# Feature rows stored twice in DRAM, a new sequence of Strassen segments and a newly written instruction order in a two-block transformer kernel

## The chip, the cores and the metric

The kernel runs on one core of one Trainium2 chip. The metric is the time of one execution in microseconds on the device; the time before is 683.48 us, the median of three runs (683.15 to 684.11).

## What is computed

One pre-norm transformer layer in float32, on 2048 tokens of 448 features:

```python
h  = x + attention(layernorm(x)) @ wo        # 16 heads of 28, causal, window of 256 tokens
h2 = h + (gelu(n @ w_gate) * (n @ w_up)) @ w_down,   n = layernorm(h)    # 1792 hidden features
```

Scores are scaled by 28 ** -0.5, masked to the 256 tokens up to the query and go through a softmax. Biases and layer-norm gains are not there.

## The kernel before, in words

**Numbers in two parts.** Matmuls run in float32r. Each operand is split in a high part (`to_hi`, line 250, a copy on ACT) and a low part (`to_lo`, line 253, the difference, on DVE or POOL), and a product is built of hi*hi, lo*hi and hi*lo terms that accumulate in one PSUM bank. Of 448 features the last 64 do not fill a block of 128 rows, so the fourth block repeats 64 rows of the third, and the spare half of it carries low parts.

**Attention.** Tokens come in 16 tiles of 128, four tiles make a chunk. Heads come in four groups, and (group, chunk) pairs make 16 attention blocks. For a block PE computes scores, DVE adds the mask and takes the maximum in one custom instruction (line 692), the maximum goes back through PE (line 719) into the operands, PE computes the transposed scores, ACT their exponential (line 766), POOL cuts the edges of the window (line 779), and PE multiplies by the values (`attend`, line 798). `output` (line 837 on) multiplies by `wo` and DVE adds into `hres` (line 845). Between these stand matmuls that wait for nothing of attention: projections of q and k, values (224 columns each), and at the end the first matmuls of the feed-forward part.

**The second layer norm.** `layer_norms` and `normalise` (lines 269 and 303) compute it per tile of 128 tokens. `turn` (line 350) transposes it: DVE turns 32 by 32 squares in place in `xn`, four DMAs (line 358) write the tile to DRAM as `xn_d[t]`, features by tokens. For tiles 0 to 7 two DMAs (lines 362, 364) load it back into `xT` and ACT, then POOL or DVE, split it.

**Feed-forward.** The hidden features come in 14 tiles of 128. Tiles 0 to 3 of the first two token chunks run as plain products (`conv`, line 1084 on; the order is `FIRST`). All others run as Strassen units: a unit takes a half of the tokens, p = 0 (chunks 0 and 1) or p = 1 (chunks 2 and 3), and one hidden tile, and does 39 matmuls of 512 columns in seven products; two `down` steps of 12 matmuls of 448 columns go with it. `SEGS` (line 30) lists the units, two hidden tiles to a segment. The token sums that the seven products need are made by `combine(p, i)` (line 415), for i = 0 to 3 in each half: DMAs (line 441) load features of two tiles from `xn_d`, DVE adds them (line 460), ACT and DVE split the sums into `xT`, `X0`, `proj` and `ring`. The weight sums are made by `record` (line 909 on): a DMA (line 930) loads one hidden tile into `raw`, POOL makes the differences (line 937), ACT, DVE and POOL split them. A record is used by all units of its hidden tile in neighbouring segments; where the two halves of the tokens follow each other on the same tiles, they share it. There are three places for records and one buffer `raw`. `down` accumulates in four PSUM banks, and when a group of `down` steps on one chunk is complete, four DVE additions (line 1069) empty the banks into `hres`; the next group on these banks waits for that.

**What sets the order.** Every engine is fed in the order of one list, `PLAN`, a compressed list of numbers that was made ahead of time from the costs and the due times (`key`) in the code; `L.play` issues the operations in that order. Each engine works through its own instructions strictly in it. SP issues all DMAs. The list also holds spare transposes of `ident` on PE (line 1306), which compute nothing that is used.

## Time and profile before

| what | value |
|---|---|
| median of 3 runs | 683.48 us |
| the profiled execution | 680.14 us |
| its span, first to last instruction | 678.4 us |
| busy: PE, DVE, ACT, POOL | 665.5, 504.8, 396.8, 299.9 us |
| instructions of PE, DVE, ACT, POOL | 4074, 1278, 765, 459 |
| mean granted TensorE clock | 0.997 |
| DMA, mean over the span | 132 GB/s |

The numbers of the profile are of one execution, which was 3.34 us shorter than the median. PE's busy time counts a matmul from its issue to its modelled end, and neighbouring matmuls overlap, so a matmul's own duration (about 380 ns for 512 columns) is longer than its distance to the next, and a short gap between two matmuls does not show as idle time.

The stages lie as follows in the span: loads and the first layer norm from 0 on, attention blocks from about 60 to 304 us, plain feed-forward products to about 360 us, Strassen units to the end.

### The profile page before, as it was taken

How to read it: one execution, taken by the hardware profiler on the slowest of the kernel's cores; microseconds unless marked ns; L12 is line 12 of the kernel's file. 1: busy time of each engine (PE TensorE's matmuls, PEld its weight loads, DVE VectorE, ACT ScalarE, POOL GpSimd, SP SyncE). 2: the span in 40 equal slices, each digit the busy share in tenths (PEclk: the TensorE clock that was granted, in tenths of full speed). 3: DMA queues.
4: the chain of work that ended last, by engine and by line, in shares of the span. 5: the costliest groups of instructions: out<-in, count | busy, mean ns of one | idle time of the engine just before them, and what ended most of it. 6: DMA issues, size and time to landing. Idle time of an engine off the chain costs nothing.

```text
span 678.4 us, 11973 instructions
## 1 busy us (share of the span) xinstructions
PE 665.5 (98%) x4074; PEld 592.7 (87%) x4074; DVE 504.8 (74%) x1278; ACT 396.8 (58%) x765; POOL 299.9 (44%) x459
## 2 busy tenths in 40 slices
PE   8999999999999999999989999999999999999997
PEld 7998878888889877778878999999999999999997
DVE  7898789977688979977988899876566355545554
ACT  5766578774867698886455655634554443433431
POOL 3632524543444488756433474256554442122200
PEclk9999999999999999999998999999999999999999
DMA  7888866464747687544534434121212201101202
GB/s 268 267 254 250 265 185 210 140 213 135 236 131 255 180 210 221 125 119 105 150 98 95 102 85 128 57 91 39 67 53 70 74 15 52 52 7 62 110 0 109
DMA packets 92951, 89.66 MB, mean 132 GB/s; under 512 B 35225, under 2 KB 82009, under 8 KB 92889
## 3 DMA queue, kind: packets, MB, share of 16 engines
q1 hardware_dynamic: 92888, 88.89, 44.2%
q8 instruction: 32, 0.52, 0.3%
q14 instruction: 31, 0.25, 0.1%
HBM read 59.51 MB, written 29.36 MB: 131 GB/s over the span
## 4 chain that ended last, share of the span: by engine, by line
PE 88%; DVE 7%; DMA 2%; issue 1%; ACT 1%; SPq 1%; POOL 0%; DVEq 0%; ACTq 0%
PE bank L248 81%; PE bank L798 6%; DVE bank L692 2%; DVE v L460 1%; DMA v<-xn 1%; PE bank L314 1%; DMA pp<-in_wv_dram 1%; DVE xT L254 1%; DVE X L254 1%; SPq L441 0%; DVE proj L254 0%; PE bank L719 0%; DVE hres L1069 0%; DVE mhl L712 0%; DVE xn L823 0%
## 5 line engine op out<-in xcount | busy, mean ns | idle before, releaser
L248 PE MATMUL bank<-xT,proj 128*128 128x512 f32 x620 | 171.1, 384 | 0.0
L692 DVE CUSTOM_DVE_ANT_0 bank<-bank,mask 128x384 f32<-128x384 f32 (+2 forms) x256 | 131.6, 551 | 24.0 <-PE bank L248 22.0
L248 PE MATMUL bank<-ring 84*128 84x384 f32 (+6 forms) x618 | 136.3, 311 | 2.4 <-DVE mx L692 1.0
L248 PE MATMUL bank<-xT,ring 128*128 128x512 f32 x536 | 134.8, 379 | 0.0
L248 PE MATMUL bank<-ring,proj 128*128 128x448 f32 x628 | 128.9, 356 | 2.5 <-DVE hres L1069 2.5
L248 PEld LDWEIGHTS bank<-ring,proj 128*128 128x128 f32 x628 | 119.6, 190 | 5.8 <-ACT xT L251 2.9
L248 PEld LDWEIGHTS bank<-xT,proj 128*128 128x128 f32 x620 | 113.6, 190 | 11.4 <-DVE mhl L709 0.2
L766 ACT ACTIVATE pp<-bank 128x384 f32<-128x384 f32 (+1 forms) x212 | 103.3, 533 | 21.6 <-PE bank L248 18.4
L248 PEld LDWEIGHTS bank<-ring 128*128 128x128 f32 (+1 forms) x618 | 103.5, 190 | 13.7 <-DVE mx L692 2.4
L248 PEld LDWEIGHTS bank<-xT,ring 128*128 128x128 f32 x536 | 101.1, 189 | 13.1 <-DVE v L1013 0.6
L779 POOL TENSOR_SCALAR_AFFINE_SELECT pp<-pp 128x512 f32<-128x512 f32 x120 | 73.9, 642 | 56.1 <-ACT pp L766 55.2
L1069 DVE TENSOR_TENSOR hres<-bank,hres 128x448 f32<-128x448 f32 x72 | 42.7, 618 | 33.0 <-PE bank L248 32.9
L248 PE MATMUL bank<-proj,xT 128*128 128x224 f32 x352 | 60.8, 274 | 0.3 <-ACT proj L251 0.2
L937 POOL TENSOR_TENSOR raw<-raw 64x128 f32<-64x128 f32 (+1 forms) x90 | 48.3, 549 | 28.7 <-DMA raw<-in_halves_dram 25.4
L254 DVE TENSOR_TENSOR proj<-v,proj 128x512 fp32r<-128x512 f32 (+1 forms) x56 | 40.2, 725 | 23.9 <-ACT proj L251 23.5
L248 PEld LDWEIGHTS bank<-proj,xT 128*128 128x128 f32 x352 | 52.9, 191 | 2.3 <-ACT proj L251 0.7
L251 ACT ACTIVATE proj<-v 128x512 fp32r<-128x512 f32 (+1 forms) x56 | 32.8, 601 | 36.0 <-DVE v L1039 32.4
L254 POOL TENSOR_TENSOR ring<-raw,ring 128x256 fp32r<-128x256 f32 (+2 forms) x42 | 38.3, 920 | 35.2 <-ACT ring L251 34.5
L251 ACT ACTIVATE ring<-bank 8x512 fp32r<-8x512 f32 x64 | 37.4, 585 | 26.8 <-PE bank L719 25.5
L1013 DVE TENSOR_TENSOR v<-v,bank 128x512 f32<-128x512 f32 x48 | 32.8, 684 | 26.2 <-PE bank L248 23.6
L248 PE MATMUL bank<-wos,ohl 128*128 128x448 f32 x192 | 49.4, 359 | 0.3 <-DVE mx L692 0.2
L248 PE MATMUL bank<-X,ring 128*128 128x512 f32 x146 | 48.2, 379 | 0.0
(117 smaller groups left out, 955.7 us busy)
## 6 DMA issues: line engine op xcount, KB each, us to landing
ring<-k SPq DMA_DIRECT2D x44, 336.0 KB
raw<-in_halves_dram SPq DMA_DIRECT2D x18, 640.0 KB
ring<-q SPq DMA_DIRECT2D x32, 336.0 KB
q<-proj SPq DMA_DIRECT2D x15, 448.0 KB
k<-proj SPq DMA_DIRECT2D x11, 448.0 KB
hres<-in_x_dram SPq DMA_DIRECT2D x16, 224.0 KB
xn<-xn SPq DMA_DIRECT2D x64, 56.0 KB
ge<-in_halves_dram SPq DMA_DIRECT2D x16, 224.0 KB
```

The lines of the kernel that those rows point to most:

```text
L248: nc.tensor.matmul(o.rearrange("p (t h) -> p t h", h=2), w, mixed(m), **how)
L251: nc.scalar.activation(dst, src, AF.Copy)
L254: (eng or nc.vector).tensor_sub(dst, src, f(hi))
L314: nc.tensor.transpose(bank[b.k][:, n * 128:(n + 1) * 128], xn[i2][:, o:o + 128], ident)
L460: op("dve", 0.07 + n * 0.00104, 0.17 + n * 0.00104, key, lambda: nc.vector.tensor_tensor(out, a, b, op=op_), [*ar, *br, "mtfree"], w, port ...
L692: nc.vector.tensor_tensor_reduce(at, at, plain(mask[:, o:384]), 1.0, -BIG, OP.add, OP.max, mx[i // 2][:, i % 2, j:j + 1])
L766: nc.scalar.activation(pp[:, j:j + per, o * 128:o * 128 + n].rearrange("p j (h t) -> p j h t", h=2), bank[b.k][:, 0:n * per].rearrange("p ...
L779: nc.gpsimd.affine_select(a, a, pattern=[[0, 4], [-cm, 128]], compare_op=op_, fill=0.0, base=0, channel_multiplier=cm)
L798: nc.tensor.matmul(bank[b.k][32 * j:32 * j + DH + 1, lo * 128:(hi + 1) * 128], v[:, 4 * c - 2 + m, g % 2, j, :], pp[:, j, at[m] * 128:(at[ ...
L937: op("pool", 0.14 + n * 0.00215, 0.18 + n * 0.00215, key, lambda: nc.gpsimd.tensor_tensor(out, a, b, op=OP.subtract), [*ar, *br], w, port= ...
L1013: op("dve", 0.605, 0.702, key, lambda: nc.vector.tensor_tensor(plain(out), plain(a), unmixed(bank[bs[i].k]), op=OP.add), ar, w, bs[i])
L1069: op("dve", 0.533, 0.626, key + 3 * q + 3, lambda t=t, b=banks[q]: nc.vector.tensor_tensor(plain(hres[:, t, :]), unmixed(bank[b.k][:, 0:D] ...
```

## The change

Five things are changed:

1. **Twice the rows.** The buffer `xn` becomes 512 wide (`xw`), and ACT writes the tile's first 64 features in front of all 448 of them, in two instructions (`norm_twice`), so that `xn_d[t]` holds 512 rows: features 0 to 63, then 0 to 447. DVE turns 512 columns. The four DMAs that write a tile have runs of the same length and 16 squares where they had 14.
2. **Loads of `combine`.** All blocks that the sums need are now plain slices of those rows: one load for the first tile of a pair, where there were three, and four for the second, where there were five. The weights' rows are laid out to fit (`four`, `turned`). In `turn` the last block goes through a small buffer `last` in `ring`, which the DMA of line 373 now writes, and ACT needs two instructions where it needed three.
3. **`SEGS`.** All ten units of the first half of the tokens come first, then the fourteen of the second. Only hidden tiles 12 and 13 are still shared, so 22 records are made where there were 18. There are fewer groups of `down` steps, so that line 1069 (now 1078) runs 64 times, not 72.
4. **Splits at the start.** The low parts of the first value weights and of the first q/k weight tile are made on POOL, where they were made on DVE.
5. **`PLAN`, due times and planner costs.** The list is a new one. `LN2` and the second entry of `XK` (the due time of the second half's sums) are later. PE has 36 spare transposes, where it had 30; its other matmuls are the same in number and size.

`MOVED` now bounds the tiles of the first layer norm that go through DRAM; at 16 there are none, so that this way is taken by the second layer norm alone, as before.

```diff
-SEGS = ((0, (4, 5)), (0, (6, 7)), (0, (8, 9)), (1, (8, 9)), (1, (6, 7)), (1, (4, 5)), (1, (0, 1)), (1, (10, 11)), (0, (10, 11)), (0, (12, 13)), (1, (12, 13)), (1, (2, 3)))
+SEGS = ((0, (4, 5)), (0, (6, 7)), (0, (8, 9)), (0, (10, 11)), (0, (12, 13)), (1, (12, 13)), (1, (10, 11)), (1, (8, 9)), (1, (6, 7)), (1, (4, 5)), (1, (0, 1)), (1, (2, 3)))
...
-LN2 = (120, 10)
-XK = ((0, 10), (240, 10))
+LN2 = (180, 10)
+XK = ((0, 10), (360, 10))
...
-    xn_d = [dram.tile([D, 128], F32, name=f"xn{t}") for t in range(NT)]
+    xn_d = [dram.tile([512, 128], F32, name=f"xn{t}") for t in range(NT)]
...
+        def norm_twice():
+            for n, o in ((64, 0), (D, 64)):
+                nc.scalar.activation(xw[i2][:, o:o + n], hres[:, t, 0:n], AF.Identity, scale=bnve[:, 1, i4:i4 + 1],
+                                     bias=bnve[:, 2, i4:i4 + 1])
...
-        dma(key + 0.1, 230, lambda: nc.sync.dma_start(f(xT[:, 4:7, c]), d[0:384].rearrange("(b p) t -> p b t", p=128)),
+        last_at = span("ring", 10240, 128)
+        dma(key + 0.1, 230, lambda: nc.sync.dma_start(f(xT[:, 4:7, c]), d[128:512].rearrange("(b p) t -> p b t", p=128)),
             put, [XT(t)])
-        dma(key + 0.1, 80, lambda: nc.sync.dma_start(f(xT[:, 3, c]), d[D - 128:D]), put, [("xt3", t)])
+        dma(key + 0.1, 80, lambda: nc.sync.dma_start(last, d[0:128]), put, [last_at])
...
-            load(slice(0, 128), 0, 2, d[0:256].rearrange("(k p) t -> p k t", k=2), 0)
-            last = d[384:448].rearrange("(k p) t -> p k t", k=1)
             if not k:
-                load(LOW, 2, 2, some(d, 2, 2), 1)
-                load(HIGH, 2, 2, some(d, 2, 3)[:, 0::2], 2)
+                load(slice(0, 128), 0, 4, d.rearrange("(k p) t -> p k t", k=4), 0)
             else:
-                load(LOW, 3, 1, some(d, 2, 2)[:, 1:2], 1)
-                load(LOW, 4, 2, some(d, 2, 2), 2)
-                load(HIGH, 4, 2, some(d, 2, 2), 3)
-                load(HIGH, 2, 2, last.to_broadcast([64, 2, 128]), 4)
+                load(slice(0, 128), 3, 3, d[128:512].rearrange("(k p) t -> p k t", k=3), 0)
+                load(slice(0, 128), 0, 1, d[0:128], 1)
+                load(HIGH, 1, 2, d[128:256].rearrange("(k p) t -> p k t", k=2), 2)
+                load(LOW, 1, 1, d[128:192], 3)
...
-            op("dve", 0.54, 0.63, key + 1, lambda b=b: to_lo(wv[:, 1, b:b + 2], wv_raw[p][:, b:b + 2], wv[:, 0, b:b + 2]),
+            eng, name = (nc.vector, "dve") if p else (nc.gpsimd, "pool")
+            op(name, 0.54 if p else 1.1, 0.63 if p else 1.15, key + 1, lambda b=b, eng=eng: to_lo(
+                wv[:, 1, b:b + 2], wv_raw[p][:, b:b + 2], wv[:, 0, b:b + 2], eng),
                [WVRAW(p, b, 2), WV(0, b, 2)], [WV(1, b, 2)], port=True)
...
 PLAN = (
-    "c-pPEW3(nc)HWEWQb-|H)wXThwr$(CZQHhO+qP|M`t3gbeBaEPHS=TU)Vh;OvT^Mzd)G-IV1NS*2%x{;!0#6Re*Zg$zgOVz2mg^lzklp^3xBsb"
...
```

What the list does to each engine's instructions is seen in their order. Tiles 0 to 15 of `xn_d` are named `xn_118` to `xn_133` there.

**SP, the loads for the third pair of tiles of the first half** (tiles 2 and 6, `xn_120` and `xn_124`), just before the plain feed-forward products end. Before:

```order
L441 DMA v<-xn_124 64x2x128
L441 DMA v<-xn_123 64x2x128
L358 DMA xn_129<-xn_85 32x14x32 x2
L441 DMA v<-xn_124 64x128
L358 DMA xn_126<-xn_80 32x14x32
L441 DMA v<-xn_120 64x2x128
L441 DMA v<-xn_124 64x2x128 x2
L441 DMA v<-xn_124 128x2x128
L441 DMA v<-xn_120 64x2x128
L441 DMA v<-xn_120 128x2x128
```

Now:

```order
L450 DMA v<-xn_124 128x128
L450 DMA v<-xn_125 128x128
L450 DMA v<-xn_124 64x2x128
L450 DMA v<-xn_124 128x3x128
L450 DMA v<-xn_124 64x128
L450 DMA v<-xn_120 128x4x128
```

Eight loads of the pair have become five, and no write of a later tile stands among them. From the first to the last load of the first half's four pairs there are 20 loads, 4 writes of tiles and 2 loads of weights, where there were 32 loads, 10 writes and 3 loads of weights; the writes of `xn_129` and `xn_128` come behind.

**DVE, up to the additions that empty the four `down` banks before the first Strassen unit** (`hres` from banks 138 to 141). Before:

```order
L460 TENSOR_TENSOR v<-v 128x128
L460 TENSOR_TENSOR v<-mask,v 128x2x128
L460 TENSOR_TENSOR v<-v 64x128 x2
L254 TENSOR_TENSOR proj<-ge,proj 128x512
L254 TENSOR_TENSOR X_3702<-v,xT 128x2x128
L460 TENSOR_TENSOR v<-v 128x128 x2
L1069 TENSOR_TENSOR hres<-bank_138,hres 128x448
L1069 TENSOR_TENSOR hres<-bank_139,hres 128x448
L1069 TENSOR_TENSOR hres<-bank_140,hres 128x448
L254 TENSOR_TENSOR X_3702<-v,xT 128x128
L254 TENSOR_TENSOR X_3702<-v,xT 128x2x128
L1069 TENSOR_TENSOR hres<-bank_141,hres 128x448
```

Now:

```order
L466 TENSOR_TENSOR v<-mask,v 128x2x128
L255 TENSOR_TENSOR proj<-ge,proj 128x512
L466 TENSOR_TENSOR v<-v 128x128
L255 TENSOR_TENSOR X_3708<-v,xT 128x2x128
L466 TENSOR_TENSOR v<-v 64x128
L255 TENSOR_TENSOR X_3708<-v,xT 128x128 x2
L255 TENSOR_TENSOR xT<-v,xT 64x128
L1078 TENSOR_TENSOR hres<-bank_138,hres 128x448
L1078 TENSOR_TENSOR hres<-bank_139,hres 128x448
L1078 TENSOR_TENSOR hres<-bank_140,hres 128x448
L1078 TENSOR_TENSOR hres<-bank_141,hres 128x448
```

The work of `combine` still stands ahead of the four additions. Between the first addition of the group before and the first of this one 74 instructions stood, and now 71: a `BN_STATS`, a `BN_AGGR`, the two transposes of the second layer norm, one split of 512 columns and one addition on 64 rows are gone from it, and one split each of 2x128 and 128 columns on 128 rows and of 128 columns on 64 rows have come in.

**PE, between the thirteenth and the fourteenth `attend`** (`bank<-ring` are scores, `bank<-proj,xT` are values of the second half of the heads, which wait for nothing of attention). Before:

```order
L248 MATMUL bank_135<-ring 128x384
L248 MATMUL bank_140<-ring 128x384
L248 MATMUL bank_134<-ring 128x384
L248 MATMUL bank_137<-ring 128x384
L248 MATMUL bank_141<-ring 128x384
L248 MATMUL bank_135<-ring 128x384
L248 MATMUL bank_136<-ring 128x384
```

Now:

```order
L249 MATMUL bank_136<-ring 128x384
L249 MATMUL bank_140<-proj,xT 128x224 x2
L249 MATMUL bank_141<-ring 128x384
L249 MATMUL bank_140<-proj,xT 128x224
L249 MATMUL bank_135<-proj,xT 128x224 x2
L249 MATMUL bank_137<-ring 128x384
L249 MATMUL bank_140<-proj,xT 128x224 x2
```

Matmuls that need nothing of attention have moved from the middle blocks to the last ones. Between the twelfth and the sixteenth `attend` stood 44 of 512 columns and 11 of 224; now there are 70 and 59.

More of the change, by code (lines that the diff above doesn't have):

```diff
@@ L169, in block_kernel @@
     one_r = pool.tile([128, 128], F32R, name="one")
[L170 removed]
+    xw = [o_m, pool.tile([128, 512], F32, name="xn1")]
+    xn.append(xw[1][:, 0:D])
     qk_d = [[[dram.tile([GF, 3, 512], F32, name=f"{'qk'[i]}{g}_{c}") for i in range(2)] for c in range(CS)]
             for g in range(NG)]
[L174 removed]
+    xn_d = [dram.tile([512, 128], F32, name=f"xn{t}") for t in range(NT)]
     bank = [psum.tile([128, 512], F32, name=f"bank{i}") for i in range(8)]
@@ L193, in block_kernel @@
     xT = xT_m.rearrange("p (b t) -> p b t", b=7)
-    last_hi = ring_m[:, 10240:10368]
+    last = f(ring_m[:, 10240:10368])
     rq_m, rk_m = ring_m[:, 0:4096], ring_m[:, 4096:10240]
@@ L256, in dma @@
     def dma(key, size, fn, r=(), w=(), after=()):
-        cost = 0.63 if size in (32, 64, 128) else 0.52 if size == 150 else 0.46 if size < 240 else 0.4
+        cost = 0.62 if size in (32, 64) else 0.52 if size in (128, 150) else 0.46 if size < 240 else 0.42
         return op("sp", cost, 0, key, fn, r, w, size=size, after=after)
@@ L303, in normalise @@
     def normalise(t, key, kind):
-        moved = kind == "ln2" and t >= MOVED
-        i2, i4 = (t % 2 if t > 7 else 1) if moved else t % 2 if t < 4 else 1, t % 4
+        moved = kind == "ln2" or t >= MOVED
+        i2, i4 = t % 2 if t < 4 and kind == "ln1" or t > 7 and kind == "ln2" else 1, t % 4
         b = None if moved else Bank(kind)
@@ L337, in normalise @@
             op("pool", 1.0, 1.1, key, norm_pool, [HR(t), ("bnve", i4)], [("xn", i2)], port=True)
+        elif moved:
+            op("act", 0.88, 0.95, key, norm_twice, [HR(t), ("bnve", i4)], [("xn", i2)])
         else:
@@ L358, in turn @@
             dma(key, 150, lambda dst=dst, src=src: nc.sync.dma_start(dst, src), [at], [("xnd", t, a)])
-        if t > 7:
+        if kind == "ln2" and t > 7:
             return
         put = [("xnd", t, a) for a in range(4)]
-        dma(key + 0.1, 230, lambda: nc.sync.dma_start(f(xT[:, 4:7, c]), d[0:384].rearrange("(b p) t -> p b t", p=128)),
+        last_at = span("ring", 10240, 128)
+        dma(key + 0.1, 230, lambda: nc.sync.dma_start(f(xT[:, 4:7, c]), d[128:512].rearrange("(b p) t -> p b t", p=128)),
             put, [XT(t)])
-        dma(key + 0.1, 80, lambda: nc.sync.dma_start(f(xT[:, 3, c]), d[D - 128:D]), put, [("xt3", t)])
-        eng = nc.gpsimd if t in TURNED else nc.vector
+        dma(key + 0.1, 80, lambda: nc.sync.dma_start(last, d[0:128]), put, [last_at])
+        on_pool = kind == "ln1" or t in TURNED
+        eng = nc.gpsimd if on_pool else nc.vector
         def hi():
             to_hi(xT[:, 0:3, c], f(xT[:, 4:7, c]))
-            to_hi(last_hi[64:128], f(xT[64:128, 3, c]))
-            to_hi(xT[0:64, 3, c], f(xT[64:128, 3, c]))
+            to_hi(xT[:, 3, c], last)
         def lo():
             to_lo(xT[:, 4:7, c], f(xT[:, 4:7, c]), xT[:, 0:3, c], eng)
-            to_lo(xT[64:128, 3, c], f(xT[64:128, 3, c]), last_hi[64:128], eng)
-        op("act", 1.1, 1.2, key + 0.2, hi, [("xt3", t)], [XT(t), span("ring", 10240, 128)])
-        op("pool" if t in TURNED else "dve", 1.6 if t in TURNED else 0.8, 1.7 if t in TURNED else 0.88, key + 0.2, lo,
-           [XT(t), span("ring", 10240, 128)], [XT(t)], port=True)
+            to_lo(xT[64:128, 3, c], last[64:128], xT[64:128, 3, c], eng)
+        op("act", 0.8, 0.9, key + 0.2, hi, [last_at], [XT(t)])
+        op("pool" if on_pool else "dve", 1.6 if on_pool else 0.8, 1.7 if on_pool else 0.88, key + 0.2, lo,
+           [XT(t), last_at], [XT(t)], port=True)
     LOW, HIGH = slice(0, 64), slice(64, 128)
@@ L431, in two @@
             return T[k].rearrange("p (b t) -> p b t", t=128)[:, n:n + step + 1:step]
-        def some(src, *ks):
-            return src[128 * ks[0]:128 * ks[0] + 64 * ks[1]].rearrange("(k p) t -> p k t", k=ks[1])
         for k in range(2):
@@ L491, in combine @@
         add(256, two(0, 0, 2), at(0, 0, 2), E, e, two(0, 0, 2), at(0, 0, 2), key + 2)
-        parts_of(4, both(1), at(1, 0, 1, 2, 3), 2, key + 2)
-        add(128, b(0, 1), at(0, 1), b(0, 1), at(0, 1), b(0, 0), at(0, 0), key + 2)
-        add(128, b(0, 3, LOW), at(0, 3), b(0, 3, LOW), at(0, 3), b(0, 2, LOW), at(0, 2), key + 2)
+        parts_of(4, both(1), at(1, 2, 3, 4, 5), 2, key + 2)
+        add(128, b(0, 3), at(0, 3), b(0, 3), at(0, 3), b(0, 2), at(0, 2), key + 2)
+        add(128, b(0, 1, LOW), at(0, 1), b(0, 1, LOW), at(0, 1), b(0, 0, LOW), at(0, 0), key + 2)
         parts_of(2, both(0), at(0, 0, 1, 2, 3), 2, key + 2)
@@ L1467, in layout @@
               for n in range(0, F, 128)]
-    ffn = [np.concatenate([rows(gate[:, n:n + 128]).reshape(128, 512), rows(up[:, n:n + 128]).reshape(128, 512),
+    ffn = [np.concatenate([turned(gate[:, n:n + 128]).reshape(128, 512), turned(up[:, n:n + 128]).reshape(128, 512),
                            inputs["B_w_down"][n:n + 128]], axis=1) for n in range(0, 128 * GC, 128)]
```

293 lines of the change are left out of this document (150 added, 143 removed).

## The prediction

> **What bounds the kernel now.** I read the busy times by stage first, in stretches of 20 us. The columns behind the stretch are its length, then the busy time of PE, PE's weight loads, DVE, ACT and POOL, the granted clock of PE, and DMA.
>
> ```profile
> core 0: us, PE busy (x) PEld busy (x) DVE busy (x) ACT busy (x) POOL busy (x), PEclk, DMA share, GB/s
> 0.00:20.00 20.00, 17.30 (x110) 15.61 (x111) 16.12 (x37) 12.06 (x18) 8.38 (x28) 1.00 0.78 264
> ...
> 200.00:220.00 20.00, 20.00 (x156) 18.36 (x156) 16.23 (x52) 15.47 (x34) 9.55 (x12) 1.00 0.72 234
> ...
> 240.00:260.00 20.00, 19.17 (x154) 16.16 (x156) 16.50 (x51) 17.32 (x36) 16.34 (x23) 1.00 0.83 224
> 260.00:280.00 20.00, 19.05 (x177) 14.28 (x177) 19.24 (x67) 18.07 (x38) 16.99 (x24) 1.00 0.77 205
> 280.00:300.00 20.00, 19.47 (x142) 16.05 (x140) 17.94 (x52) 17.12 (x37) 11.93 (x22) 1.00 0.48 114
> ...
> 340.00:360.00 20.00, 17.46 (x81) 15.67 (x80) 18.09 (x49) 10.95 (x20) 6.58 (x10) 0.94 0.29 76
> 360.00:380.00 20.00, 20.00 (x94) 17.79 (x93) 14.86 (x29) 11.53 (x21) 9.52 (x15) 0.98 0.46 107
> ...
> 440.00:460.00 20.00, 20.00 (x100) 18.49 (x99) 15.71 (x26) 8.69 (x17) 11.74 (x18) 1.00 0.25 78
> 460.00:480.00 20.00, 20.00 (x99) 18.36 (x98) 11.94 (x19) 9.71 (x19) 13.99 (x21) 1.00 0.14 46
> ...
> 660.00:680.00 20.00, 14.38 (x75) 13.64 (x73) 9.01 (x15) 2.27 (x4) 0.00 (x0) 0.96 0.24 93
> ```
>
> PE has next to no room. Its idle time is 2.70 us at the start, 20 - 14.38 = 5.62 us in the last row, of which 1.6 us lies behind the span's end at 678.4 and 4.02 us before it, 2.54 us between 340 and 360, and 0.83 + 0.95 + 0.53 = 2.31 us between 240 and 300. A change that leaves PE's matmuls as they are can give only what lies in the middle of these. The chain of work that ended last says the same of the end: from 356.59 us on it is PE alone.
>
> ```profile
> 356.59 316.48 PE bank L248 x1529
> 673.09 1.69 DVE hres L1069 x3
> ```
>
> So I looked at the stall in front of it in stretches of 3 us, and then at who was late there, on DVE's timeline (start, duration, instruction, idle time before it).
>
> ```profile
> 354.00:357.00 3.00, 0.46 (x3) 0.44 (x3) 3.00 (x9) 1.86 (x4) 1.56 (x1) 1.00 0.00 0
> 357.00:360.00 3.00, 3.00 (x12) 2.72 (x11) 2.97 (x7) 1.89 (x4) 0.72 (x1) 0.58 0.07 22
> 360.00:363.00 3.00, 3.00 (x14) 2.59 (x13) 2.94 (x8) 1.74 (x3) 0.89 (x1) 0.85 0.00 0
> ```
>
> ```profile
> 324.39 0.62 DVE L1069 TENSOR_TENSOR hres<-bank,hres 128x448 f32<-128x448 f32 x1
> ...
> 328.15 0.75 DVE L460 TENSOR_TENSOR v<-v 128x256 f32<-128x256 f32 x2 [0.35 <-DMA v<-xn]
> ...
> 344.43 0.42 DVE L254 TENSOR_TENSOR X<-v,xT 128x256 fp32r<-128x256 f32 x1 [0.96 <-ACT xT L251]
> ...
> 347.14 0.69 DVE L1115 TENSOR_TENSOR ge<-bank,ge 128x512 f32<-128x512 f32 x1 [0.59 <-ACT ge L1112]
> ...
> 355.83 1.67 DVE L1069 TENSOR_TENSOR hres<-bank,hres 128x448 f32<-128x448 f32 x3
> ```
>
> PE waits 2.54 us for the four additions of line 1069, because DVE does the token sums of `combine` first. Behind it the clock is at 0.58 for 3 us and at 0.85 for another 3, which loses 3 x 0.42 + 3 x 0.15 = 1.71 us. The whole stall costs 2.54 + 1.71 = 4.25 us. The chain goes through SP's issues and the landing of the loads here, and SP's timeline shows why.
>
> ```profile
> 324.46 0.60 SPq L441
> 325.11 0.59 SPq L441
> 325.75 2.38 DMA v<-xn
> ```
>
> ```profile
> 319.44 2.55 SPq L441 DMA_DIRECT2D v<-xn  x4
> ...
> 333.12 4.51 SPq L441 DMA_DIRECT2D v<-xn  x7
> ...
> 341.53 4.32 SPq L441 DMA_DIRECT2D v<-xn  x7
> ...
> 348.40 0.36 SPq L930 DMA_DIRECT2D raw<-in_halves_dram  x1
> ...
> 367.82 0.35 SPq L930 DMA_DIRECT2D raw<-in_halves_dram  x1
> ...
> 382.07 0.35 SPq L930 DMA_DIRECT2D raw<-in_halves_dram  x1
> ...
> 395.56 0.36 SPq L930 DMA_DIRECT2D raw<-in_halves_dram  x1
> ...
> 407.71 0.33 SPq L930 DMA_DIRECT2D raw<-in_halves_dram  x1
> ```
>
> A load takes about 0.62 us of SP (4.51 / 7 = 0.64, 4.32 / 7 = 0.62), so that the 32 loads of the first half's sums are 20 us of SP's time ahead of the last of these sums.
>
> **The loads and the stall before the units.** In the new order 20 loads stand there: 12 x 0.62 = 7.4 us less on SP, and 6 writes and one weight load fewer between them. The last sums can start some 7 us sooner, so DVE is what decides. From the addition at 324.39 to that at 355.83 DVE takes 31.44 us. What leaves this stretch and what comes in is priced by these groups.
>
> ```profile
> L284 DVE BATCH_NORM_STATS2 bnst<-hres 128x6 f32<-128x448 f32 x32 | 19.4, 617 | 1.7 <-DMA hres<-in_x_dram 1.4
> L354 DVE STREAM_TRANSPOSE xn<-xn 128x448 f32<-128x448 f32 x16 | 10.2, 638 | 0.8 <-ACT xn L309 0.8
> L254 DVE TENSOR_TENSOR proj<-ge,proj 128x512 fp32r<-128x512 f32 x6 | 4.3, 724 | 0.0
> L254 DVE TENSOR_TENSOR X<-v,xT 128x256 fp32r<-128x256 f32 x28 | 11.7, 429 | 1.1 <-ACT xT L251 1.0
> ```
>
> Out go 0.62 + 2 x 0.64 + 0.72 = 2.62 us, in comes 0.43 us; of the smaller ones two go and two come, which I set against each other. That makes 31.44 - 2.19 = 29.25 us. The idle 0.35 + 0.96 + 0.59 = 1.90 us in the stretch is what late loads and ACT cause, so 27.35 us if all of it goes. PE is held up no more if DVE takes 31.44 - 2.54 = 28.90 us. The two ends lie on both sides of that, by 0.35 us to the bad and 1.55 us to the good; I take the stall as gone. A rest of 0.35 us would not cost clock: the stretch from 240 to 260 us has 0.83 us of idle at a clock of 1.00. The Trainium skill's page TensorE: Matmul & The Clock Gate, Part 1: The HAM clock gate, says that the clock is halved after an idle window of about 3.4 us. By that page a wait of 2.54 us would cost no clock, and the sum would be 1.71 us poorer; the trace has the clock at 0.58 behind it, and the measurement decides. **-4.25 us**, between -3.9 and -4.25.
>
> **Filling the last attention blocks.** Between 240 and 300 us DVE is busy 53.7 of 60 us and PE idles for 2.31 us. By the new order 26 more matmuls of 512 columns and 48 more of 224 stand between the twelfth and the sixteenth `attend`. At 100 matmuls of mostly 512 and 448 columns in 20 us, and half of that for 224 columns, this is 26 x 0.2 + 48 x 0.1 = 10 us of PE work that waits for nothing, many times the idle 2.31. It is missing in the blocks before; one of their stretches, from 200 to 220 us, has PE at 20.00 and DVE at 16.23. At best more than 2.31 us comes back, as gaps shorter than a matmul's record don't show; at worst the idle time moves to the middle blocks and nothing comes back. I take the shown **-2.31 us**.
>
> **Spare transposes.** Six more, priced by seven at the start:
>
> ```profile
> 7.25 0.93 PE L1306 MATMUL bank<-ident 128*128 128x128 f32 x7
> ```
>
> 6 x 0.13 = **+0.8 us** if all lie where PE is busy, nothing if they lie in waits; I take the dear end.
>
> **Splits on POOL at the start.** Two of 448 columns and one of 512.
>
> ```profile
> L254 DVE TENSOR_TENSOR proj<-pp,proj 128x448 fp32r<-128x448 f32 x2 | 1.3, 626 | 0.1
> L254 POOL TENSOR_TENSOR wos<-raw,wos 128x448 fp32r<-128x448 f32 x4 | 4.6, 1145 | 5.2 <-ACT wos L251 5.2
> ```
>
> POOL takes 0.52 us longer for one, so PE, which wants the low parts after seven matmuls with the high ones, could wait 3 x 0.52 = 1.6 us; DVE is freed of 3 x 0.63 = 1.9 us in a stretch in which it is busy 16.12 of 20 us, while POOL has 11.6 us to spare. From -1.9 to +1.6, I take **0**, since neither is shown to end a wait.
>
> **Work beside PE.** `norm_twice` adds a short ACT instruction per tile and line 368's function loses one, DVE turns 64 columns more; none is near PE's chain after 360 us. Eight fewer additions of line 1069 free DVE there. The four records more are the one thing that could reach PE (third rival); in the stretches from 440 to 480 us, where one record goes with each unit, POOL is at 11.74 and 13.99 of 20 us and PE at 20.00. **0**. Later sums of the second half lighten DVE between 360 and 430 us, which covers nothing that PE waits for.
>
> **The sum.** -4.25 - 2.31 + 0.8 = -5.76, so 680.14 - 5.76 = 674.4 us for an execution like the profiled one. That one is 3.34 us under the median, with nothing in the trace to say why; I carry this over: 683.48 - 5.76 = **677.7 us**. Changes within 0.2% (1.4 us) a measurement of this kernel can hardly tell from none.
>
> **The rivals.**
> - **The stall stays on DVE.** The order still has nearly all of `combine` ahead of the four additions: 71 instructions where there were 74. For it: DVE was idle for 1.90 us only of 31.44. Against it: the 2.19 us that are gone from the stretch. If half a microsecond of the wait goes and the clock falls all the same: -0.5 - 2.31 + 0.8 = -2.0, 681.5 us. Chance 0.15, of which 0.04 within the bound.
> - **The idle time moves within attention.** Ten microseconds of filler are taken from the middle blocks. Nothing comes back: -4.25 + 0.8 = -3.45, 680.0 us. Chance 0.15. Both together: -0.5 + 0.8, 683.8 us, no change. Chance 0.07.
> - **Records fall behind the units: slower.** Ten units in a row now need a new record each, where the first six did. The loads of `raw`, issued once the record before is done with it, stand at 367.82, 382.07, 395.56, 407.71: 14.25, 13.49 and 12.15 us apart. A unit with its `down` steps is 63 matmuls at 0.2 us, 12.7 us. If records keep the 13.9 us of the first two intervals, four more fall 4 x 1.2 = 4.9 us behind, in two waits of about 2.5 us that each cost 1.71 us of clock as well: 8.3 us, and 677.7 + 8.3 = 686.0 us. It decides once the intervals stay over 12.7 us. Against it: DVE, on which the records' splits wait, has less of `combine` to do there. Chance 0.13.
>
> That the loads or segments are not what they say can't be: the built order has 40 loads for 64 and 22 records for 18.
>
> **How the numbers follow.** The forecast has the remaining 0.50. Faster: 0.50 + 0.11 + 0.15 = 0.76; same: 0.04 + 0.07 = 0.11; slower: 0.13. The range goes up to 683.8, the case of no gain, and leaves the record case out. Below, all idle time between 20 and 360 us could go and some that doesn't show: the forecast less 1.9 us at the start, 0.8 us of transposes and some 3 us in gaps that are hidden, 672.0 us.
>
> **What would show it.** Right: PE at 3.00 of 3 us in the stretches around the first unit, the clock at 1.00 there, the additions in front of it no later than PE's last matmul, loads on SP ending well ahead of the sums, DVE less full and PE fuller between the twelfth and the sixteenth block. Wrong: DVE still full up to those additions, waits of PE on DVE's line 701 in the middle blocks, or PE waiting on ACT or POOL writing `ring` or `proj` between 390 and 490 us, with loads of `raw` over 13 us apart.

## The result, and the profile after

The changed kernel takes 675.45 us (median of 4 runs, 674.98 to 677.31) against 683.32 us (682.15 to 684.11, 4 runs): a ratio of 0.9891, 95% interval 0.9867 to 0.9916. Its profiled execution took 674.99 us with a span of 673.3 us, 5.15 us less than the one before. With the experiments the kernel before was run again and had medians of 681.8 (18 runs), 681.99 (17) and 681.41 us (12); against these the changed kernel's 675.45 us is 6.0 to 6.5 us less. The changed kernel was not run again there, so its variants are compared with it by their ratios to the kernel before, each known to about 0.002, which is 1.4 us.

The busy times by stage, with the columns of the prediction's first fence:

```profile
0.00:20.00 20.00, 17.41 (x107) 15.65 (x107) 15.02 (x32) 11.53 (x18) 12.72 (x31) 1.00 0.76 258
...
200.00:220.00 20.00, 20.00 (x150) 18.35 (x146) 17.47 (x54) 13.22 (x27) 9.34 (x12) 1.00 0.68 210
...
240.00:260.00 20.00, 20.00 (x157) 17.93 (x155) 16.89 (x48) 16.43 (x35) 15.14 (x21) 1.00 0.76 211
260.00:280.00 20.00, 19.22 (x156) 15.90 (x156) 15.44 (x51) 18.57 (x40) 15.06 (x24) 1.00 0.86 225
280.00:300.00 20.00, 19.94 (x139) 15.81 (x138) 17.11 (x52) 15.02 (x34) 11.52 (x18) 1.00 0.37 92
...
340.00:360.00 20.00, 19.97 (x97) 17.83 (x96) 18.54 (x49) 10.15 (x20) 5.27 (x9) 1.00 0.23 69
360.00:380.00 20.00, 20.00 (x97) 18.06 (x97) 14.76 (x26) 12.94 (x25) 9.84 (x18) 1.00 0.56 134
...
660.00:680.00 20.00, 8.72 (x47) 8.36 (x45) 6.33 (x11) 0.94 (x2) 0.00 (x0) 0.94 0.24 92
```

The stall has gone: between 340 and 360 us PE idles for 0.03 us, not 2.54, and the clock is at 1.00 there and behind. Between 240 and 300 us the idle time is 0.78 + 0.06 = 0.84 us, not 2.31. The chain of waits now has PE alone from 305.48 us on, where it began at 356.59:

```profile
305.48 25.79 PE bank L249 x126
331.31 21.32 PE bank L249 x102
352.66 314.75 PE bank L249 x1529
667.43 1.69 DVE hres L1078 x3
```

The additions in front of the first unit, on DVE's timeline (line 1069 is 1078 now), with the idle time of DVE between the first addition of the group before and the four of this group:

```profile
323.68 1.14 DVE L1078 TENSOR_TENSOR hres<-bank,hres 128x448 f32<-128x448 f32 x2
...
342.15 0.63 DVE L255 TENSOR_TENSOR X<-v,xT 128x128 fp32r<-128x128 f32 x2 [0.38 <-ACT xT L252]
...
346.83 0.29 DVE L255 TENSOR_TENSOR X<-v,xT 128x128 fp32r<-128x128 f32 x1 [0.25 <-ACT xT L252]
...
351.89 2.22 DVE L1078 TENSOR_TENSOR hres<-bank,hres 128x448 f32<-128x448 f32 x4
```

Between these two marks DVE takes 351.89 - 323.68 = 28.21 us, where it took 31.44; this time is called the stretch from here on. DVE's idle time in it is 0.63 us, where it was 1.90, and its busy time (the third of the busy times in these rows, the kernel before first) 27.07 us, where it was 28.97:

```profile
324.39:355.83 31.44, 29.41 (x142) 26.35 (x140) 28.97 (x74) 15.38 (x29) 12.47 (x18) 1.00 0.46 123
323.68:351.89 28.21, 28.17 (x137) 25.45 (x136) 27.07 (x72) 15.42 (x31) 7.75 (x12) 1.00 0.26 77
```

The additions are only just in time. The first one ends at 352.52 us and PE's next matmul starts at 352.66, 0.15 us later, as it does in the profiles of e4, e7, e8, e9 and e10, also where their timelines name a write of ACT as what PE waited for. It starts 0.39 us after the matmul before it, where its neighbours stand 0.19 us apart.

The loads on SP (line 450) and the records' loads (line 939):

```profile
321.75 19.92 SPq L450 DMA_DIRECT2D v<-xn  x13
...
364.46 0.35 SPq L939 DMA_DIRECT2D raw<-in_halves_dram  x1
...
376.75 0.34 SPq L939 DMA_DIRECT2D raw<-in_halves_dram  x1
389.93 0.36 SPq L939 DMA_DIRECT2D raw<-in_halves_dram  x1
404.46 0.35 SPq L939 DMA_DIRECT2D raw<-in_halves_dram  x1
416.35 0.34 SPq L939 DMA_DIRECT2D raw<-in_halves_dram  x1
```

The last thirteen loads of the first half are spread over 20 us with gaps between them. The records' loads stand 12.3, 13.2, 14.5 and 11.9 us apart from 364 us on, and PE is at 20.00 in the stretches there.

### The profile page after: what moved, and what is told of

It is laid out like the page before. It is cut to its first block, busy times and chain, and to the rows that moved or that the text cites. A ratio compares the mean times of both kernels' runs of the same rounds, so it can differ in the third digit from the quotient of the medians.

```text
span 673.3 us, 12063 instructions
## 1 busy us (share of the span) xinstructions
PE 664.0 (99%) x4080; PEld 592.8 (88%) x4080; DVE 512.1 (76%) x1287; ACT 406.3 (60%) x793; POOL 322.6 (48%) x506
## 4 chain that ended last, share of the span: by engine, by line
PE 95%; DVE 2%; DMA 1%; ACT 1%; issue 0%; POOL 0%; SPq 0%; DVEq 0%
PE bank L249 87%; PE bank L807 6%; PE bank L320 1%; DVE bank L701 1%; DMA hres<-in_x_dram 1%; DMA raw<-in_wqk_dram 1%; ACT pp L775 0%; PE bank L728 0%; DVE hres L1078 0%; PE bank L1315 0%; POOL proj L255 0%; ACT proj L252 0%; ACT ring L252 0%; DVE xn L835 0%; SPq L510 0%
## 5 line engine op out<-in xcount | busy, mean ns | idle before, releaser
L249 PE MATMUL bank<-xT,proj 128*128 128x512 f32 x648 | 181.9, 386 | 0.2 <-ACT proj L252 0.2
L249 PE MATMUL bank<-ring 128*128 128x384 f32 (+7 forms) x629 | 139.9, 311 | 1.4 <-DVE mx L701 1.2
L249 PEld LDWEIGHTS bank<-xT,proj 128*128 128x128 f32 x648 | 118.1, 190 | 13.2 <-issue 0.6
L249 PE MATMUL bank<-xT,ring 128*128 128x512 f32 x508 | 127.5, 379 | 0.0
L249 PEld LDWEIGHTS bank<-xT,ring 128*128 128x128 f32 x508 | 95.9, 189 | 12.4 <-ACT ge L1121 0.4
L946 POOL TENSOR_TENSOR raw<-raw 64x128 f32<-64x128 f32 (+1 forms) x110 | 53.5, 498 | 35.5 <-DMA raw<-in_halves_dram 31.3
L249 PE MATMUL bank<-proj,xT 128*128 128x224 f32 x352 | 69.8, 272 | 0.0
L249 PEld LDWEIGHTS bank<-proj,xT 128*128 128x128 f32 x352 | 58.2, 191 | 1.9 <-ACT v L252 0.2
L255 POOL TENSOR_TENSOR ring<-raw,ring 128x256 fp32r<-128x256 f32 (+2 forms) x48 | 41.8, 878 | 34.8 <-ACT ring L252 32.3
L1078 DVE TENSOR_TENSOR hres<-bank,hres 128x448 f32<-128x448 f32 x64 | 37.5, 617 | 14.8 <-PE bank L249 14.7
```

The lines of the kernel that those rows point to most:

```text
L249: nc.tensor.matmul(o.rearrange("p (t h) -> p t h", h=2), w, mixed(m), **how)
L255: (eng or nc.vector).tensor_sub(dst, src, f(hi))
L946: op("pool", 0.14 + n * 0.00215, 0.18 + n * 0.00215, key, lambda: nc.gpsimd.tensor_tensor(out, a, b, op=OP.subtract), [*ar, *br], w, port= ...
L1078: op("dve", 0.533, 0.626, key + 3 * q + 3, lambda t=t, b=banks[q]: nc.vector.tensor_tensor(plain(hres[:, t, :]), unmixed(bank[b.k][:, 0:D] ...
```

## The experiments

**What sets the stall.** The theory is the prediction's: DVE's work in the stretch is what has to fit into PE's time. The rivals are the place of the four additions alone, and SP's loads alone.

`e1_adds_first`: the kernel before, with another order on DVE only (its rows, from the built order):

```
+L254 TENSOR_TENSOR proj<-ge,proj 128x512
 L460 TENSOR_TENSOR v<-v 64x128 x2
...
 L460 TENSOR_TENSOR v<-mask,v 128x2x128
+L1069 TENSOR_TENSOR hres<-bank_138,hres 128x448
+L1069 TENSOR_TENSOR hres<-bank_139,hres 128x448
+L1069 TENSOR_TENSOR hres<-bank_140,hres 128x448
+L1069 TENSOR_TENSOR hres<-bank_141,hres 128x448
 L460 TENSOR_TENSOR v<-v 64x128 x2
-L254 TENSOR_TENSOR proj<-ge,proj 128x512
...
-L1069 TENSOR_TENSOR hres<-bank_138,hres 128x448
```

> The kernel before, with its four additions of line 1069 ahead of the first unit moved six places forward on VectorE (and the last low part of the ninth feed-forward step before them, since the next matmuls read it). Theory (all of VectorE's work up to the first unit is late, not just the additions): the additions are in time, PE passes 353.7 without its 2.54 us wait, but the sums that were passed over are what the unit reads from its ninth matmul on, and VectorE is done with them at about 362 as before; PE waits there instead, 2.5 to 3.2 us. Time within 1 us of the kernel before, ratio 0.9985 to 1.0015. Rival (the place of the additions alone): the wait and its clock loss go, 4.25 us less, ratio 0.994, and no other wait appears.

685.05 us, ratio 1.0045 (1.0029 to 1.0062): slower. PE's timeline, which is some 4 us later here than in the profile before:

```profile
358.80 2.51 PE L248 MATMUL bank<-ring,proj 128*128 128x448 f32 x12 [1.07 <-DVE hres L1069]
361.14 1.03 PE L248 MATMUL bank<-xT,proj 128*128 128x512 f32 x4
362.01 0.38 PE L248 MATMUL bank<-X,proj 128*128 128x512 f32 x1
362.42 1.13 PE L248 MATMUL bank<-xT,proj 128*128 128x512 f32 x4
365.49 0.70 PE L248 MATMUL bank<-X,proj 128*128 128x512 f32 x2 [1.94 <-DVE X L254]
```

The additions still cost 1.07 us, and then the first unit waits 1.94 us after its ninth matmul for the sums that were passed over, 3.01 us together where 2.54 were. The rival falls. The time came out worse than the theory said, and most of that arises ahead of the rows that were moved: by the starts of the same matmuls in both profiles this execution is 3.91 us behind the profile before at 320 us already, 1.7 us of it by a stretch at half clock at 274 us. From 320 to 390 us it loses 1.36 us more. Why it came later up to 320 us is not shown; the instructions and their order are the same there, yet none of the six executions was under 684 us.

`e2_three_loads_out`: the kernel before with 40 loads.

```diff
+                skip = (k, part) in ((0, 2), (1, 1), (1, 4))
-                dma(key, (64 if rows.stop - rows.start == 128 else 32) * n, lambda: nc.sync.dma_start(
+                dma(key, (64 if rows.stop - rows.start == 128 else 32) * n, lambda: skip or nc.sync.dma_start(
```

> The kernel before with three of the eight loads of every pair of token sums left out (three sums read old data), so 40 loads for 64, in the old order. Theory (VectorE's own work decides): at most the 1.90 us that VectorE idled in the stretch come back, the wait in front of the first unit is still 0.6 us or more, 0 to 2.5 us less, ratio 0.9963 to 1. Rival (SyncE's loads decide): the stall goes as in the changed kernel, 4.25 us less, ratio 0.994 or under.

680.86 us, ratio 0.9987 (0.9969 to 1.0004). The additions come 30.65 us after the first one, not 31.44:

```profile
324.84 0.62 DVE L1070 TENSOR_TENSOR hres<-bank,hres 128x448 f32<-128x448 f32 x1 [0.30 <-PE bank L248]
...
355.49 1.67 DVE L1070 TENSOR_TENSOR hres<-bank,hres 128x448 f32<-128x448 f32 x3
```

PE waits 1.67 us. So the loads alone are worth 0.8 us of DVE's stretch, and no difference in time that this measurement resolves. The theory holds, and SP's loads alone do not decide.

`e3_eight_loads`: the changed kernel with 64 loads.

```diff
+                def go(out=out, src=src, n=n):
+                    if n < 3:
+                        nc.sync.dma_start(out, src)
+                        return
+                    for c in (slice(0, 2), *(slice(m, m + 1) for m in range(2, n))):
+                        nc.sync.dma_start(out[:, c], src[:, c])
-                dma(key, (64 if rows.stop - rows.start == 128 else 32) * n, lambda: nc.sync.dma_start(out, src), put,
+                dma(key, (64 if rows.stop - rows.start == 128 else 32) * n, go, put,
```

> The changed kernel with each pair's two large loads cut into three and two, so eight loads again for five, same bytes, same order. Theory: SyncE has idle time among these loads in the new order, VectorE stays in time to within its margin; 0 to 0.7 us more, ratio 1.000 to 1.001 against the changed kernel (0.989 to 0.990 against the kernel before). Rival (the loads were the gain): the 2.5 us wait comes back with its clock loss, 4.25 us more, ratio to the kernel before 0.995.

675.23 us, ratio 0.9897 (0.9876 to 0.9918): as the changed kernel. The stretch is 353.33 - 325.06 = 28.27 us. In the new order eight loads do as well as five.

`e7_lighter_dve`: the kernel before with less of DVE's work.

```diff
-        op("dve", 0.56, 0.65, key, lambda: nc.vector.transpose(xb, xb), [at], [at], port=True)
+        m = 64 if t in (10, 13) else D
+        op("dve", 0.56, 0.65, key, lambda: nc.vector.transpose(xb[:, 0:m], xb[:, 0:m]), [at], [at], port=True)
...
+            out = p == 0 and i > 1
-            sub(128, lambda: hi[HIGH, 0, 1], src[HIGH, 0, 1], hi[HIGH, 0, 1], [*r, *w[1]], XS(p, q, 1, i), key, 0.1)
+            sub(128, lambda: hi[HIGH, 0, 1], src[HIGH, 0, 1], hi[HIGH, 0, 1], [*r, *w[1]], XS(p, q, 1, i), key, 0.1, out)
```

> The kernel before with some 2.9 us of VectorE's work left out of the stretch ahead of the first unit, all 64 loads and the order as they are: two transposes of 448 columns are cut to 64 columns (0.53 us less each) and the six small subtractions of 64 rows of the third and fourth pair of the first half are left out (about 0.3 us each), so that the sums and some normalised rows are wrong. Theory (VectorE's work ahead of the additions sets the stall): PE's wait of 2.54 us falls to 0 to 0.5 us, the half clock behind it goes, 2.0 to 4.3 us less, ratio 0.994 to 0.997. Rival (loads or ScalarE set it): the wait stays above 2 us, ratio 0.999 to 1.

680.41 us, ratio 0.998 (0.9964 to 0.9996). The stretch is 354.44 - 324.62 = 29.82 us, and PE waits 1.05 us:

```profile
324.62 0.62 DVE L1071 TENSOR_TENSOR hres<-bank,hres 128x448 f32<-128x448 f32 x1
...
354.44 1.67 DVE L1071 TENSOR_TENSOR hres<-bank,hres 128x448 f32<-128x448 f32 x3
```

```profile
324.62:354.44 29.82, 29.52 (x144) 26.69 (x142) 27.24 (x72) 15.62 (x29) 10.82 (x18) 1.00 0.48 126
```

The wait lies between the theory's 0.5 us and the rival's 2 us. The edit took less out of the stretch than was meant: DVE is busy for 27.24 us there, 1.73 us less, not 2.9. Each of the two transposes became 0.41 us shorter (0.64 to 0.23 us), and only three of the six small subtractions stand in the stretch. Of these 1.73 us 1.62 came back. The miss is in the size of the edit, not in the mechanism.

`e9_loads_and_dve`: the edits of e2 and e7 together.

> The kernel before with both: three of eight loads of every pair left out, and the 2.9 us of VectorE's work ahead of the first unit left out (sums and some normalised rows are wrong). Alone they took 0.7 and 1.3 us off PE's wait of 2.54 us; VectorE still idled about 1.5 to 2 us for ScalarE. Theory (both feed one row of VectorE work that is late): together the wait falls to 0.6 us or less, no half clock behind it, 2.5 to 4 us less, ratio 0.994 to 0.9965. Rival (a third thing of the new order is needed, ScalarE's place or an earlier begin of the sums): more than 0.6 us of wait is left, ratio 0.997 or more.

678.25 us, ratio 0.9948 (0.9926 to 0.997), in the range that the theory gave. The stretch is 29.62 us (additions at 325.12 and 354.74), and 0.70 us of wait is left before the additions, 0.80 with a short one behind, a little more than the 0.6 us set. So the ratio is the theory's and the wait is on the rival's side: what still differs from the new order is mostly DVE's idle time for ACT, 0.95 + 1.00 us here and 0.63 us there. The mean clock was 0.999 or 1.000 in all seven executions.

`e10_heavier_dve`: the changed kernel with 1.6 us more on DVE.

```diff
+                def go():
+                    for _ in range(2 if out is E and not p else 1):
+                        nc.vector.tensor_tensor(out, a, b, op=op_)
```

> The changed kernel with the first addition of each of the four pairs of the first half made twice (same result), 4 x 0.41 us = 1.6 us more on VectorE ahead of the first unit. Theory (VectorE has no room there): the four additions come 0.9 to 1.6 us later and PE waits for them that long, without half clock, ratio to the kernel before 0.9905 to 0.992. Rival (there is room): no wait over 0.3 us, ratio as the changed kernel's, 0.989 to 0.990.

676.64 us, ratio 0.9928 (0.9913 to 0.9944): a little above the theory's 0.992, which the interval takes in, and outside the rival's range. The stretch grew by 0.74 us to 28.95, since DVE's idle time of 0.63 us took up part of the new work, and PE waits 0.39 us at 333 us and 0.48 us for the four additions:

```profile
325.67 1.14 DVE L1081 TENSOR_TENSOR hres<-bank,hres 128x448 f32<-128x448 f32 x2
...
354.62 2.22 DVE L1081 TENSOR_TENSOR hres<-bank,hres 128x448 f32<-128x448 f32 x4
```

`e4_adds_late` and `e4a_adds_little_late`: the changed kernel with its four additions five and three instructions later on DVE. The rows of the second:

```
-L1078 TENSOR_TENSOR hres<-bank_138,hres 128x448
...
 L255 TENSOR_TENSOR X_3708<-v,xT 128x2x128
 L1124 TENSOR_TENSOR ge<-bank_136,ge 128x512
 L255 TENSOR_TENSOR xT<-mask,xT 64x128
+L1078 TENSOR_TENSOR hres<-bank_138,hres 128x448
```

> The changed kernel with its four additions of line 1078 ahead of the first unit moved five instructions back on VectorE, which makes them some 2.3 us late. Theory: PE waits 2.0 to 2.5 us and the clock falls behind the wait as in the kernel before, together 3.5 to 4.3 us more than the changed kernel, ratio to the kernel before about 0.995. By the Trainium skill's page TensorE: Matmul & The Clock Gate, Part 1, a wait this short costs no clock: 2.0 to 2.5 us more, 0.9925. If instead the stall was worth all of the 7.9 us between the medians, because timed executions lose more clock there than the profiled one, about 7 us more, ratio 0.999 to 1.

> The changed kernel with its four additions ahead of the first unit moved three instructions back on VectorE, where e4 had five. Theory (half clock follows when PE idles for more than about 1.85 us of one of the fixed stretches of 3.41 us): PE waits 1.2 to 1.6 us, no half clock behind it in any execution, 1.2 to 1.6 us more than the changed kernel, ratio to the kernel before 0.991 to 0.992. Rival (any wait of a microsecond or more can halve the clock): half clock at 357 us in some executions, 1.7 us more there, ratio up to 0.994.

679.06 us, ratio 0.9957 (0.9937 to 0.9977), and 675.98 us, ratio 0.9919 (0.9906 to 0.9932). On PE's timeline the first waits 2.97 us and the second 1.56 us; the clock behind the wait is at 0.50 in the first and at 1.00 in the second (rows in the last section):

```profile
355.40 2.80 PE L249 MATMUL bank<-ring,proj 128*128 128x448 f32 x10 [2.97 <-DVE hres L1078]
```

```profile
353.64 2.51 PE L249 MATMUL bank<-ring,proj 128*128 128x448 f32 x12 [1.56 <-DVE hres L1078]
```

Both came out as their theories say, the first with a longer wait; its interval leaves out both a loss of about 7 us and one without any loss of clock. Three of its seven executions kept a mean clock of 0.999, with 677.88 to 678.41 us, so the same order does not always lose the clock. The second kept 0.999 or more in all five.

In the order before, the stretches 31.44, 30.65, 29.82 and 29.62 us go with waits of 2.54, 1.67 to 1.93, 1.05 to 1.15 and 0.70 to 0.80 us (the larger figures count short waits behind, too): the wait is what the stretch has over some 28.9 us. In the new order that limit is some 28.1 us: e4's stretch of 31.03 us (323.62 to 354.65) less its wait is 28.06, e4a's 29.74 (323.13 to 352.87) less 1.56 is 28.18, and e10's 28.95 less 0.39 and 0.48 is 28.08. Part of the difference is where DVE begins: its first addition starts 4.13 us after the 24 matmuls `bank<-proj` before it have begun on PE (319.55 us), and 3.63 us after them (320.76 us) in the kernel before. With 28.21 us the additions have no room to spare.

**The last attention blocks.** The theory is that the matmuls moved there run in PE's waits.

`e11_fewer_fillers`: most of the moved matmuls for the values are left out.

```diff
+            short = p == 1 and t > 9
-            op("pe", mm(224), 0.29, key + a / 16, lambda a=a, h=h, wb=wb, xb=xb: mul(
+            op("pe", mm(224), 0.29, key + a / 16, lambda a=a, h=h, wb=wb, xb=xb, short=short: short and a > 0 or mul(
...
-                stop=(a == NP - 1)), [XT(t), WV(h, wb)], () if a else [V(t)], b, tag="v")
+                stop=short or a == NP - 1), [XT(t), WV(h, wb)], () if a else [V(t)], b, tag="v")
```

> The changed kernel without 60 of the 66 matmuls of 224 columns that the values of the last six tiles of the second pass need (these values are wrong); they stand between the eleventh and the fourteenth attend, at 0.097 us each 5.8 us of PE work. Theory (they fill waits there): PE waits again, 1.5 to 2.5 us more than the changed kernel, so only 3.3 to 4.3 us are saved, less if a half clock follows: ratio to the kernel before 0.983 to 0.987. Rival (they fill nothing, PE is the bound there anyway): 5.5 to 5.8 us saved, ratio 0.981 or less.

674.88 us, ratio 0.9909 (0.989 to 0.9929). Of the 5.8 us of PE work that is gone nothing shows in the ratio. The span of the profiled execution is 1.4 us shorter (671.9 for 673.3), but by the starts of the same matmuls it is 0.70 us ahead before the first of those left out, near 233 us, and 1.37 us at the end, so 0.7 us are left. The waits are back, 1.36 + 1.12 + 0.24 = 2.72 us for 0.84:

```profile
240.00:260.00 20.00, 18.64 (x133) 14.91 (x132) 17.28 (x48) 15.50 (x34) 14.56 (x22) 1.00 0.83 223
260.00:280.00 20.00, 18.88 (x133) 13.76 (x132) 16.00 (x56) 19.65 (x43) 16.52 (x23) 1.00 0.81 212
280.00:300.00 20.00, 19.76 (x136) 15.34 (x135) 15.41 (x46) 14.43 (x34) 11.04 (x18) 1.00 0.41 104
```

The theory holds, more strongly than it was put: these matmuls are nearly free where they stand. The waits that show account for 1.9 of the 5.1 us that were not saved; that the rest lies in gaps too short to show is argued. One of the six executions had a mean clock of 0.994 and one 0.997, so some lost clock, too.

`e5_no_late_spares`: the changed kernel without the five late spare transposes.

```diff
-                warm(w - n)
+                if len(done) < 2000:
+                    warm(w - n)
```

> The changed kernel without the five spare transposes that stand in the last attention blocks (two near 271 us, three near 302 us); the 31 at the start stay. By the forecast's price of 0.13 us each: 0.65 us less, ratio to the kernel before 0.988. Theory now: what they cost is hidden or about 0.07 us each, and they fill stretches in which PE is short of work; without them more executions get a stretch of 3.41 us at half clock there, 1.7 us each: from 0.5 us less (no such stretch) to 1.2 us more (one in every execution), and lower mean clocks than the changed kernel's 0.997 to 1.000 (ratio 0.988 to 0.991).

674.81 us, ratio 0.9897 (0.9883 to 0.9912): no difference from the changed kernel that the times resolve, and 0.65 us would be within the interval. The two profiles say more: by the starts of the same matmuls the one without the five is 0.09 us ahead at 239 us and 0.12 us ahead at 390 us, so that in this pair they cost 0.03 us. Three of four executions had a mean clock of 0.999 or more, as three of four of the changed kernel had, so no guarding of the clock shows either.

**The start, and the records.**

`e6_splits_on_dve`: the changed kernel with the three low parts of the first weights on DVE again.

```diff
-            eng, name = (nc.vector, "dve") if p else (nc.gpsimd, "pool")
+            eng, name = nc.vector, "dve"
...
-        eng, name = (nc.vector, "dve") if m else (nc.gpsimd, "pool")
+        eng, name = nc.vector, "dve"
```

> The changed kernel with the three low parts of the first weights back on VectorE, as the kernel before has them, in the new order. The forecast took this term as 0, with bounds of 1.6 us less (if PE now waits for GpSimd) and 1.9 us more (if VectorE is what PE waits for at the start). Theory: within 0.5 us of the changed kernel, ratio to the kernel before 0.988 to 0.990. Rival: the start depends on it, and PE's first 20 us hold 1 us more or less of idle time.

675.85 us, ratio 0.9907 (0.9893 to 0.9921). The interval takes in the changed kernel's ratio; a cost of up to 1 us can't be excluded. PE's busy time in the first 20 us can't decide it: in the profiles of the new order it lies between 15.68 (e10) and 17.54 us (e11), with the same instructions at the start. At 100 us e6's matmuls start 0.12 us later than the changed kernel's, and those of e3, e4, e4a, e8 and e10 between 1.13 us earlier and 0.34 us later. The profiled execution of e6 is its slowest, 680.78 us with a mean clock of 0.992: it has a stretch at half clock at 118 us and two, one behind the other, at 272 us.

`e8_slower_records`: the changed kernel with more of POOL's work in each record.

```diff
+            def go():
+                for _ in range(2 if out is E else 1):
+                    nc.gpsimd.tensor_tensor(out, a, b, op=OP.subtract)
```

> The changed kernel with the first difference of every record computed twice on GpSimd (same result), about 0.55 us more per record. Third rival's mechanism (records pace the units): the first six records are ready only as the units read them, so 2 to 3.3 us of waits appear between 370 and 430 us, perhaps with half clock behind them, ratio to the kernel before 0.992 to 0.996. If the records have room (GpSimd is idle for 10 of 20 us there): no more than 0.5 us, ratio 0.989 to 0.990.

675.79 us, ratio 0.9917 (0.99 to 0.9933), between the two ranges that were given. PE has no wait that shows from 370 to 430 us, where the records were to pace the units (its matmuls come 0.30 us later there by their starts); it has one of 0.64 us in front of the first unit:

```profile
352.00:355.00 3.00, 2.36 (x13) 2.04 (x12) 2.96 (x9) 1.94 (x4) 1.19 (x2) 1.00 0.00 0
...
370.00:400.00 30.00, 30.00 (x145) 26.82 (x144) 26.00 (x41) 18.64 (x37) 18.63 (x29) 1.00 0.36 93
400.00:430.00 30.00, 30.00 (x148) 27.65 (x147) 23.68 (x47) 16.21 (x31) 18.34 (x30) 1.00 0.39 105
```

That wait comes from DVE's stretch again, which is 28.71 us (324.24 to 352.95). While POOL works on the longer record, two of DVE's instructions take 0.92 and 1.22 us, where the same two take 0.43 and 0.69 us in the changed kernel:

```profile
348.79 1.61 POOL L948 TENSOR_TENSOR v<-raw 128x256 f32<-128x256 f32 x2 [10.74 <-DMA raw<-in_halves_dram]
```

```profile
348.89 0.92 DVE L466 TENSOR_TENSOR v<-mask,v 128x256 f32<-128x256 f32 x1
349.74 1.22 DVE L255 TENSOR_TENSOR proj<-ge,proj 128x512 fp32r<-128x512 f32 x1
```

So the records have room for about 0.55 us each, and what they cost here goes by way of DVE. No version beat the changed kernel by more than the measurement resolves.

## Why the prediction was right, and where it was not

The direction and the range were right; the forecast of 5.76 us stands against 7.87 between medians and against 5.15 between profiled executions. In the profiled pair the first unit's matmuls behind the stall start 3.93 us earlier (352.66 for 356.59 us), the 1529 matmuls from there on take 1.73 us less (314.75 for 316.48 us), and some 0.5 us are lost behind the last matmul.

- **The stall, -4.25: right in the profiled pair, with less room than was thought.** The wait of 2.54 us and the halved clock are both gone. DVE's stretch was put at 27.35 to 29.25 us and is 28.21: its busy time fell by 1.90 us, where 2.19 were forecast, and 1.27 of the 1.90 us of idle time went. That both DVE's own work and its waits for late data count is shown by e2, e7 and e9. What failed is the limit: the 28.90 us hold in the old order (the stretch less the wait is 28.98, 28.77 and 28.92 us in e2, e7 and e9), but the prediction took them over to the new one, where the limit is some 28.1 us. A stretch of 28.9 us, within the prediction's bounds, would have left about 0.8 us of wait; that nothing is left is partly luck. The clock's 1.71 us are not in every execution: 16 of 47 of the kernel before ran at a mean clock of 0.999 or more. That five loads for eight bring the gain was not claimed, and e3 shows that in the new order they don't.
- **Late attention, -2.31: right in mechanism, too large.** 1.47 us of visible idle time came back, and between 20 and 240 us PE idles 1.18 us, where it idled 0.83. e11 shows that the moved matmuls run nearly free.
- **Spare transposes, +0.8: too dear in the profiled pair.** Leaving out five of the six gave 0.03 us in e5's profile; the times leave it open.
- **Splits 0, work beside PE 0:** not contradicted.
- **The rivals.** The stall did not stay on DVE; between 80 and 120 us PE idles 0.88 us, where it idled 0.82. Records did not pace the units: over the first half's units the loads of `raw` stand 13.0 us apart in the mean, several over 13 us, which the prediction had named as a sign against it, and yet PE shows no wait; e8 slows the records without a wait there.
- **The step that failed in the sum** is the 3.34 us between the profiled execution and the median, which I carried over to the changed kernel. That kernel's profiled execution is 0.46 us under its median. Two things differ between executions. First, the profile before was a lucky one: other profiles with the same order up to 240 us have waits that it lacks. e2 has this row, e1 and e9 have 19.39 and 19.43 there, e7 has 20.00 as the profile before, and the changed kernel 20.00:

```profile
200.00:220.00 20.00, 19.19 (x151) 17.40 (x150) 15.31 (x49) 14.51 (x32) 9.04 (x12) 1.00 0.73 225
```

By the starts of the same matmuls e1, e2, e7 and e9 are 1.89, 1.05, 0.58 and 0.79 us behind the profile before at 240 us, ahead of their edits, 1.1 us in the mean. The variants of the changed kernel that kept full clock up to there (e3, e4, e4a, e5, e8, e10) lie within 1.12 us on either side of its profile, in the mean 0.2 us ahead.

Second, how often the clock is halved differs between executions. One such stretch of 3.41 us costs 1.7 us, 0.25% of the mean clock. Of 47 executions of the kernel before, 16 have a mean clock of 0.999 or more, 22 about 0.997 (one stretch) and 9 less. With its one stretch the profile before is an ordinary execution here; the changed kernel's profile has none. Of 13 of the new order without the wait (the changed kernel, e3, e5), 10 have 0.999 or more and 3 have 0.997. As an estimate that is 40 / 47 x 1.7 - 3 / 13 x 1.7 = 1.1 us more on average before, and 0.9 us with the five executions of e6, one of which has three stretches. The profiled pair's 5.15 us, with 1.7 us of clock replaced by 1.1, and 1.1 + 0.2 us for the first point, make 5.9 us, as an estimate, of the 6.0 to 7.9 us between medians. Where the rest comes from is open.

## What to carry to other kernels

Where an engine has work to finish between two marks of another, compare the lengths of the two stretches: the wait is their difference, and moving one instruction within the row can just move the wait (e1). Read the limit again in the new order, since it moves with the marks: here it went from 28.9 to 28.1 us. Work that waits for nothing is nearly free in a stretch that another engine bounds, so look there first when an order is made. And before the difference between a profiled execution and a median is carried over, look at several profiles for what varies: it may be what the change removes.
